# Normalizing one token block from its channel-major copy instead of transposing it

## The chip, the cores and the metric

The kernel runs on one core of a Trainium2 chip. The metric is the device time of one execution in microseconds; a kernel's time is the median over its runs. The engines are called TensorE (PE), VectorE (DVE), ScalarE (ACT), GpSimd (POOL) and SyncE (SP, which issues the transfers).

## What is computed

The input `x` has 2048 tokens of 640 channels. Everything is float32.

```python
xn = layernorm(x)                       # per token, over the 640 channels
qkv = xn @ wqkv                         # 32 heads of 20
phi_q = concat(softmax(q@w_phi), softmax(-(q@w_phi)));  phi_k the same from k
o = phi_q @ (phi_k.T @ v) / (phi_q @ sum(phi_k) + 1e-6)
out = x + o @ wo + (gelu(layernorm(xn) @ w1 + b1) @ w2 + b2)
```

The MLP has 1728 hidden features. It normalizes `xn` once more, so a token's row `x - mean` is multiplied by one factor for the MLP (called `ry` in the kernel) and by another for the attention.

## The kernel before

To keep float32 accuracy, each operand of a large product is split into a high part (rounded to float32r) and a low part (the rest), and a product is three matmuls: high by high, high by low, low by high. This is `mm3`, lines 64 to 66 of the profile; `split` (lines 55, 57 and 58) makes the parts, the high one mostly on ACT, the low one on DVE or POOL.

The 2048 tokens are four blocks of 512. The kernel begins with the MLP of blocks 0 and 1. For a block `b`, `y[b]` holds the normalized tokens with channels on the 128 partitions: five chunks of 512 columns, each as a high and a low part. The weights come in 14 groups of 128 hidden features, `wc[c]` for the first four; a call of `passes(g, b, ...)` takes two such groups (j = 0 and 1) and one block through the MLP:
- its first half, `first`: for each j five `mm3` (chunks `kc` of `y[b]`) into one bank of the matmul memory, then GELU on ACT into `gts` (tile m4) and the split of the result into `hh` and `hl`;
- its second half: for m = 0 to 4 two `mm3` (`w2` parts by `hh`, `hl`) into one of banks 5, 6, 7 in turn, and DVE adds that bank to `acc[b][:, m]`, which was loaded with the residual `x` with channels on partitions (line 295 in group 0, with a bias, else 297).

The order of work at the start is written out by hand; TensorE, DVE, ACT and POOL each execute their instructions in program order. The tokens of blocks 0 and 1 are loaded as eight tiles `x0`, `x1` of 128 tokens by 640 channels. DVE takes mean and variance (`stats`, lines 130 to 154; `mv` holds means, `ry` the factors). ACT subtracts the mean (`centre`, line 158), DVE or ACT multiplies by the factor (`scale`, lines 162 and 164), and `make_y01` transposes each 128x128 piece on TensorE (line 173) into a bank that is then split into `y`. Block 0 goes first in two halves of 256 tokens: `half_first` (line 336) multiplies each half by the first two weight groups as soon as it is there, and `zs` are the four half GELUs that follow, whose results are `hid` of `p00`.

Then the passes are interleaved, so that TensorE always has a product that depends on nothing recent: `p10` (group 1, block 0) first half, `p00` (group 0, block 0) second half, `p01` (group 0, block 1) first half, `p10` second half, and so on. `p01` is the first to read `y[1]`.

A generator `mlp.beside` is advanced by one step after each `mm3`. Here it is `next_y`: after the ninth product group of `p10` it makes `y[1]` from `x1`, one transposed bank for each two further steps, so its 20 transposes stand in groups of 4, 4, 2, 4, 4, 2 among the matmuls of `p10` and `p00`. The `w2` parts of weight groups 0 and 1 are made just before (`parts[c][1]`: high part on DVE, low part on POOL), those of groups 2 and 3 behind `p00` (ACT and POOL).

Of the kernel before, what the change touches and what calls it, by code (L numbers as in the profile page):

```python
# [8 lines left out]
F32 = mybir.dt.float32  # L9
F32R = mybir.dt.float32r  # L10
AF = mybir.ActivationFunctionType
ALU = mybir.AluOpType
# [3 lines left out]
P = 128  # L16
S, D, F, H, DH = 2048, 640, 1728, 32, 20
KC = D // P
# [22 lines left out]
def f(ap):  # L41
    return ap.bitcast(F32)
# [3 lines left out]
def tile_kernel(ctx: ExitStack, tc: tile.TileContext, x, xT, wkT, wqT, wv, wphi, wo, w1, b1, w2, b2,  # L46
                ident, mmask, emask, vsel, out):
    nc = tc.nc
    ctx.enter_context(nc.allow_low_precision(reason="float32 operands are split exactly into float32r parts"))

    def split(hi, lo, src, scale=None, eng=nc.vector, first=nc.scalar):

        if scale is None:
            if first is nc.scalar:
                nc.scalar.activation(hi, src, AF.Copy)  # L55
            else:
                first.tensor_copy(hi, src)
            eng.tensor_tensor(lo, src, f(hi), op=ALU.subtract)  # L58
        else:
            nc.scalar.activation(hi, src, AF.Copy, scale=scale)  # L60
            nc.vector.scalar_tensor_tensor(lo, src, scale, f(hi), op0=ALU.mult, op1=ALU.subtract)
# [8 lines left out]
    idt = cp.tile([P, P], F32, name="idt")  # L70
# [3 lines left out]
    mv = cp.tile([P, 16, 2], F32, name="mv")  # L74
    ry = cp.tile([P, 16], F32, name="ry")
# [14 lines left out]
    acc = [None] * NB  # L90
# [6 lines left out]
    class Banks:  # L97

        def __init__(self, *ids):
            self.ids, self.n = ids, 0  # L100
# [11 lines left out]
    def mtile(i, dtype=F32):  # L112
        return mp.tile([P, 2, D if i < 5 else 512], dtype, name=f"m{i}")
    y = {}

    def load_x(ts, xp, tag="xb"):
        xbs = []
        for t in ts:
            xb = xp.tile([P, D], F32, name=tag)
            nc.sync.dma_start(xb, x[t * P:(t + 1) * P, :])  # L120
            xbs.append(xb)
        return xbs

    def stats(ts, xp, xbs, turned=False):

        t0, n = ts[0], len(ts)
        st = xp.tile([P, n, 2, 6], F32, name="st", bufs=2)
        for i, (t, xb) in enumerate(zip(ts, xbs)):
            for h in range(2):
                nc.vector.bn_stats(st[:, i, h, :], xb[:, h * 320:(h + 1) * 320])  # L130
            nc.vector.bn_aggr(mv[:, t, :], st[:, i, :, :])
            yield


        ts = slice(t0, t0 + n)
        q = xp.tile([P, 2, n], F32, name="q", bufs=2)
        nc.vector.tensor_scalar(q[:, 1, :], mv[:, ts, 1], 0.25 * (1 + EPS), 0.25 * EPS * EPS, op0=ALU.mult, op1=ALU.add)
        nc.vector.tensor_scalar(q[:, 0, :], mv[:, ts, 1], 0.25, 0.25 * EPS, op0=ALU.mult, op1=ALU.add)
        yield

        sr = xp.tile([P, 2, n], F32, name="sr", bufs=2)
        rr = xp.tile([P, 2, n], F32, name="rr", bufs=2)
        nc.scalar.activation(sr, q, AF.Sqrt)
        nc.vector.reciprocal(rr, sr)
        nc.vector.tensor_tensor(rr, rr, q, op=ALU.mult)
        if turned:
            nc.vector.scalar_tensor_tensor(sr, sr, -1.0, rr, op0=ALU.mult, op1=ALU.subtract)
        else:
            nc.vector.tensor_tensor(sr, sr, rr, op=ALU.add)
        nc.vector.reciprocal(ry[:, ts], sr[:, 1, :])  # L150
        yield
        ra = xp.tile([P, n], F32, name="ra", bufs=2)
        nc.vector.reciprocal(ra, sr[:, 0, :])
        nc.vector.tensor_tensor(rs_all[:, ts], sr[:, 1, :], ra, op=ALU.mult)

    def centre(t, xb):

        nc.scalar.activation(xb, xb, AF.Identity, bias=mv[:, t, 0:1], scale=-1.0)

    def scale(t, xb, act=False):  # L160
        if act:
            nc.scalar.activation(xb, xb, AF.Copy, scale=ry[:, t:t + 1])
        else:
            nc.vector.tensor_scalar_mul(xb, xb, ry[:, t:t + 1])

    def make_y01(b, half, xbs, ptile):

        cols = slice(half * 256, half * 256 + 256)
        for c0, n in ((0, 2), (2, 2), (4, 1)):
            ps = ptile()  # L170
            for c in range(n):
                for i in range(2):
                    nc.tensor.transpose(ps[:, c * 256 + i * P:c * 256 + (i + 1) * P],
                                        xbs[i][:, (c0 + c) * P:(c0 + c + 1) * P], idt)
            src = ps[:, :n * 256].rearrange("p (c t) -> p c t", c=n)
            cs = slice(c0, c0 + n)
            split(y[b][0][:, cs, cols], y[b][1][:, cs, cols], src)
            yield
# [20 lines left out]
    class Mlp:  # L199
        def __init__(self, slots, hid):  # L200
            self.hid, self.turn, self.slots, self.beside, self.raw = hid, 0, slots, iter(()), {}
            self.ph, self.px, self.po = Banks(0, 1, 2), Banks(3, 4), Banks(5, 6, 7)

        def fetch(self, c, pool=None):

            for p in self.fetch_parts(c, pool):
                p()
# [42 lines left out]

        def gelu(self, g, j, pz, gt, hh, hl):
            self.last = nc.scalar.activation(gt, pz, AF.Gelu_apprx_tanh, bias=b1t[:, 2 * g + j:2 * g + j + 1]).ins  # L252
            split(hh, hl, gt)

        def passes(self, g, b, ws, hid=None):

# [48 lines left out]
    mlp = Mlp((0, 1, 2, 3), ((0, 2), (1, 3)))  # L305

    def finish(p):
        for _ in p:
            pass

    xs = ExitStack()
    xp = xs.enter_context(tc.tile_pool(name="x01", bufs=8, side="right"))
# [12 lines left out]
    gts = mtile(4)  # L325
    hid = [mtile(2 * j + 1, F32R) for j in range(2)]
    hid = [(h[:, 0, :512], h[:, 1, :512]) for h in hid]
    pall = Banks(5, 6, 7, 3, 4, 0, 1, 5, 2, 6)

    def half_first(half, *order):  # L330

        cols = slice(half * 256, half * 256 + 256)
        pz = [pall()[:, cols] for _ in range(2)]
        for j, wi, yi in order:
            for kc in range(KC):
                nc.tensor.matmul(pz[j], wc[j][wi][:, kc, :], y[0][yi][:, kc, cols],
                                 start=(wi, yi, kc) == (0, 0, 0), stop=(yi, kc) == (1, KC - 1))
        return [lambda j=j: mlp.gelu(0, j, pz[j], *[m[:, cols] for m in (gts[:, j, :512], *hid[j])]) for j in range(2)]

    x1 = load_x(range(4, 8), xp)  # L340
# [14 lines left out]
    s01, s23, s47 = (stats(range(a, b), xp, xbs, True) for a, b, xbs in ((0, 2, x0[:2]), (2, 4, x0[2:]), (4, 8, x1)))  # L355

    def step(gen, n):
        for _ in range(n):
            next(gen, None)
# [22 lines left out]
    scale(2, x0[2])  # L382
    scale(3, x0[3], True)
    zs = half_first(0, *((j, wi, yi) for j in range(2) for wi, yi in ((0, 0), (1, 0), (0, 1))))
    parts[2][0]()
    step(s47, 2)
    step(y23, 4)
    zs += half_first(1, *((j, wi, yi) for ops in (((0, 0), (1, 0)), ((0, 1),)) for j in range(2) for wi, yi in ops))
    for i in range(2):
        centre(4 + i, x1[i])  # L390
    parts[3][0]()
    step(s47, 2)
    step(s01, 1)
    step(s47, 1)
    step(s47, 1)
    for i in range(2, 4):
        centre(4 + i, x1[i])
    for c in range(2):
        parts[c][1](nc.vector)
    for i in range(4):  # L400
        scale(4 + i, x1[i])
        zs[i]()
    for st in (s23, s47):
        step(st, 1)
    p00 = mlp.passes(0, 0, [wc[0], wc[1]], hid)
    next(p00)

    def next_y():
        ptile = Banks(3, 4, 0, 1)
        for _ in range(8):  # L410
            yield
        for half in range(2):
            for _ in make_y01(1, half, x1[2 * half:2 * half + 2], ptile):
                for _ in range(2):
                    yield

    mlp.beside = next_y()
    p10 = mlp.passes(1, 0, [wc[2], wc[3]])
    next(p10)
    finish(p00)  # L420
    for c in range(2, 4):
        parts[c][1]()
    finish(mlp.beside)
    p01 = mlp.passes(0, 1, [wc[0], wc[1]])
    next(p01)
    finish(p10)
# [179 lines left out]
    ptile = Banks(0, 1, 2)  # L606
# [19 lines left out]
    def proj(t, i):  # L626

        yh, yl = y[t // 4]
        c = slice((t % 4) * P, (t % 4) * P + P)
        c0 = CB[i - 1] if i else 0  # L630
        wh, wl = [w[:, :, c0:CB[i]] for w in wkv_] if i < 3 else wq_
        ps = ptile()[:, :wh.shape[2]]
        for kc in range(KC):
            mm3(ps, yh[:, kc, c], yl[:, kc, c], wh[:, kc], wl[:, kc], kc == 0, kc == KC - 1)
        return ps
# [107 lines left out]
    for t, i in [(t, i) for t in range(13) for i in range(4)] + [(13, 0), (13, 1), (13, 2), (14, 0), (14, 1), (13, 3), (14, 2), (15, 0), (15, 1),  # L743
# [6 lines left out]
        ps = proj(t, i)  # L750
# [23 lines left out]
        if i == 0 and t in (1, 2, 3, 6, 7):  # L774

            kc = (1, 2, 3, 6, 7).index(t)
# [7 lines left out]
        if (t, i) == (11, 0):  # L784
            mlp = Mlp((0, 2, 3, 1), ((1, 2), (0, 3)))
# [313 lines left out]
    for g in range(7):  # L1099
        for b in range(2, 4):  # L1100
# [24 lines left out]
            if (g, b) == (0, 3):  # L1125
# [5 lines left out]
                op = ctx.enter_context(tc.tile_pool(name="oB", bufs=1, reuse_waits="tile"))  # L1131
# [55 lines left out]
    step = 0  # L1187
# [133 lines left out]
```

## Time and profile before

| | |
|---|---|
| median of 3 runs | 726.24 us (725.75 to 726.45) |
| the profiled execution: its own time | 725.59 us |
| its span | 723.8 us |
| TensorE busy | 715.3 us, 99% of the span |
| DVE, ACT, POOL busy | 488.0, 333.5, 387.5 us |
| granted TensorE clock | 0.998 of full speed |

An engine's busy time is the time in which it had an instruction under way. In the timeline rows below, the first number is the start in microseconds from the span's start, the second how long the instruction (or a run of like ones) took from start to end; a successor on the same engine may start a little before that end. Behind `x` stands the count. The note in brackets, where there is one, is the idle time of that engine before the row and what ended it.

### The profile page before, as it was taken

The page shows a single profiled execution, that of the slowest core. Times are in us where ns is not written, and L with a number is a line of the kernel's source. Part 1 is how long each engine was busy: PE and PEld are TensorE (multiplying, and loading weights), DVE is VectorE, ACT ScalarE, POOL GpSimd, SP SyncE. Part 2 cuts the span into 40 slices and gives each one's busy share as a digit, 9 for nine tenths or more (in the row PEclk, how much of TensorE's full clock was granted, in tenths as well). Part 3 has the DMA queues.
Part 4 walks back from the last instruction along what each step waited for, and adds up shares of the span by engine and source line. Part 5 has one row for each costly group of instructions (what it writes and reads, how often), then busy time and mean ns, then how long its engine had stood idle before and what let it go on. Part 6 is the DMA issues. An engine that isn't in the chain of part 4 may idle for free.

```text
span 723.8 us, 9764 instructions
## 1 busy us (share of the span) xinstructions
PE 715.3 (99%) x3428; PEld 600.6 (83%) x3428; DVE 488.0 (67%) x821; ACT 333.5 (46%) x567; POOL 387.5 (54%) x342
## 2 busy tenths in 40 slices
PE   8999999999999999999999999999999999999998
PEld 6788888878888888888888888878878888888887
DVE  7847655765544798798788797535565656869753
ACT  7624445433313563463454458336555656551310
POOL 2211222555102896896888878346576786554400
PEclk9999999999999999999999999999999999999999
DMA  9903675555151223624500606873434443163222
GB/s 325 273 21 112 188 203 188 167 185 174 56 219 73 95 74 151 173 91 152 139 1 15 167 1 203 215 205 114 126 107 121 122 142 112 41 230 123 80 81 88
DMA packets 67145, 96.86 MB, mean 134 GB/s; under 512 B 14656, under 2 KB 37840, under 8 KB 65472
## 3 DMA queue, kind: packets, MB, share of 16 engines
q1 hardware_dynamic: 66808, 96.23, 42.9%
q8 instruction: 27, 0.44, 0.2%
q14 instruction: 22, 0.18, 0.1%
q10 hardware_dynamic: 288, 0.01, 0.0%
HBM read 65.87 MB, written 30.35 MB: 133 GB/s over the span
## 4 chain that ended last, share of the span: by engine, by line
PE 85%; DVE 4%; DMA 4%; issue 2%; ACT 2%; POOL 2%; SPq 1%; POOLq 0%; ACTq 0%
PE bank L64 25%; PE bank L65 25%; PE bank L66 25%; PE bank L704 2%; DMA r<-in_w 2%; PE bank L467 2%; PE bank L932 1%; PE bank L931 1%; DMA e<-e 1%; DVE st L130 1%; SPq L737 1%; PE bank L293 1%; PE bank L292 1%; PE bank L273 1%; PE bank L274 1%
## 5 line engine op out<-in xcount | busy, mean ns | idle before, releaser
L58 POOL TENSOR_TENSOR w<-r,w 128x640 fp32r<-128x640 f32 x52 | 84.1, 1636 | 120.0 <-ACT w L55 88.1
L64 PE MATMUL bank<-y,w 128*128 128x512 f32 (+1 forms) x310 | 121.2, 391 | 0.0
L65 PE MATMUL bank<-y,w 128*128 128x512 f32 (+1 forms) x310 | 120.7, 390 | 0.0
L66 PE MATMUL bank<-y,w 128*128 128x512 f32 (+1 forms) x310 | 120.7, 389 | 0.0
L64 PE MATMUL bank<-m,w 128*128 128x512 f32 x266 | 105.7, 397 | 1.1 <-DVE acc L295 0.6
L66 PE MATMUL bank<-m,w 128*128 128x512 f32 x266 | 104.1, 391 | 0.0
L65 PE MATMUL bank<-m,w 128*128 128x512 f32 x262 | 102.4, 391 | 0.0
L58 DVE TENSOR_TENSOR m<-m,m 128x512 fp32r<-128x512 f32 (+1 forms) x54 | 44.9, 832 | 73.8 <-ACT m L55 73.8
L297 DVE TENSOR_TENSOR acc<-bank,acc 128x512 f32<-128x512 f32 x120 | 80.4, 682 | 16.1 <-PE bank L66 11.4
L64 PE MATMUL bank<-wkh,y 128*128 128x512 f32 (+2 forms) x240 | 87.6, 365 | 0.0
L65 PE MATMUL bank<-wkl,y 128*128 128x512 f32 (+2 forms) x240 | 87.1, 363 | 0.0
L66 PE MATMUL bank<-wkh,y 128*128 128x512 f32 (+2 forms) x240 | 86.8, 362 | 0.0
L65 PEld LDWEIGHTS bank<-y,w 128*128 128x128 f32 x310 | 58.7, 189 | 12.3
L66 PEld LDWEIGHTS bank<-y,w 128*128 128x128 f32 x310 | 58.6, 189 | 12.1
L64 PEld LDWEIGHTS bank<-y,w 128*128 128x128 f32 x310 | 58.5, 189 | 12.1
L669 POOL TENSOR_TENSOR m<-m,mx 128x640 f32<-128x640 f32 (+2 forms) x48 | 44.6, 943 | 42.7 <-DVE mx L657 42.7
L650 ACT ACTIVATE m<-bank 128x512 f32<-128x512 f32 (+1 forms) x64 | 26.5, 440 | 85.5 <-PE bank L66 59.6
L925 POOL TENSOR_TENSOR e<-e,m 120x512 fp32r<-120x512 f32 (+1 forms) x28 | 38.0, 1360 | 45.0 <-ACT m L924 44.4
L64 PEld LDWEIGHTS bank<-m,w 128*128 128x128 f32 x266 | 50.0, 188 | 14.3 <-DVE acc L297 3.0
L252 ACT ACTIVATE m<-bank,b1t 128x512 f32<-128x512 f32 (+1 forms) x54 | 36.3, 672 | 52.6 <-PE bank L66 50.1
L66 PEld LDWEIGHTS bank<-m,w 128*128 128x128 f32 x266 | 49.9, 188 | 10.6
L65 PEld LDWEIGHTS bank<-m,w 128*128 128x128 f32 x262 | 49.3, 188 | 10.0
(213 smaller groups left out, 1469.3 us busy)
## 6 DMA issues: line engine op xcount, KB each, us to landing
r<-in_w SPq DMA_DIRECT2D x52, 320.0 KB
e<-e SPq DMA_DIRECT2D x40, 240.0 KB
e<-acc SPq DMA_DIRECT2D x52, 160.0 KB
acc<-in_xT SPq DMA_DIRECT2D x4, 1280.0 KB
xb<-in_x SPq DMA_DIRECT2D x8, 320.0 KB
t<-in_x SPq DMA_DIRECT2D x8, 320.0 KB
raw<-in_xT SPq DMA_DIRECT2D x10, 256.0 KB
yh<-t SPq DMA_DIRECT2D x10, 256.0 KB
```

The costliest lines, as they stand in the source:

```text
L58: eng.tensor_tensor(lo, src, f(hi), op=ALU.subtract)
L64: nc.tensor.matmul(ps, lh, rh, start=first, stop=False, **kw)
L65: nc.tensor.matmul(ps, lh, rl, start=False, stop=False, **kw)
L66: nc.tensor.matmul(ps, ll, rh, start=False, stop=last, **kw)
L130: nc.vector.bn_stats(st[:, i, h, :], xb[:, h * 320:(h + 1) * 320])
L252: self.last = nc.scalar.activation(gt, pz, AF.Gelu_apprx_tanh, bias=b1t[:, 2 * g + j:2 * g + j + 1]).ins
L297: nc.vector.tensor_tensor(acc[b][:, m, :], pw, acc[b][:, m, :], op=ALU.add)
L467: nc.tensor.matmul(ps[:, c + i * kd:c + (i + 1) * kd], raw[n, g][:kk, (kc + i) * P:(kc + i + 1) * P], wpt[:kk, g, :kd // DF, 1:], start=Tr ...
L650: return nc.scalar.activation(p3[:, :, c], ps.rearrange("p (h f) -> p h f", h=H), AF.Copy).ins
L669: subs[n, t] = nc.gpsimd.tensor_tensor(ep[:, s], a, b, op=ALU.subtract)
L704: nc.tensor.matmul(kvp[g // 2][:VM, (g % 2) * 240:(g % 2) * 240 + 240].rearrange("p (s f) -> p s f", s=4), v[:, g * VS:g * VS + VM], ft[:, ...
L925: nc.gpsimd.tensor_tensor(pl, e, f(ph), op=ALU.subtract)
```

## The change

Block 1 is no longer centred, scaled and transposed from `x1`. Its residual copy `acc[1]` already has channels on partitions, so only the 512 means and the 512 factors have to be spread over all partitions. `spread` does this with four transposes: it transposes a column of 128 tokens' values, repeated 128 times, which gives 128 equal rows. ACT copies the spread means to `mb`; POOL takes `ts[c] = mb - acc[1][:, c]` (`minus`); DVE multiplies by the spread factors in bank 2 (`times`) and ACT makes the high part; the low part (`rest`) is made on DVE for chunks 0 to 2 and on POOL for 3 and 4. `minus(0)` stands on POOL ahead of the low parts of `w2` of weight groups 0 and 1, the other four behind them. The half GELUs `zs` follow the first product on DVE. The low parts of `p10`'s two GELU results are held back (`mlp.held`) until `p00` is almost done. Both halves of `half_first` now share banks 3 and 4, and `p01` leaves out bank 2.

```diff
@@ class Mlp
+            self.held = None
@@ gelu
-            split(hh, hl, gt)
+            if self.held is None:
+                split(hh, hl, gt)
+            else:
+                nc.scalar.activation(hh, gt, AF.Copy)
+                self.held.append(lambda: nc.vector.tensor_tensor(hl, gt, f(hh), op=ALU.subtract))
@@ the start
-    pall = Banks(5, 6, 7, 3, 4, 0, 1, 5, 2, 6)
+    pall = Banks(5, 6, 7, 0, 1, 5)
+    zbanks = [Banks(n)() for n in (3, 4)]
@@ half_first
-        pz = [pall()[:, cols] for _ in range(2)]
+        pz = [z[:, cols] for z in zbanks]
@@ after the second half_first
-    for i in range(2):
-        centre(4 + i, x1[i])
     parts[3][0]()
     step(s47, 2)
+    def spread(bank, cols):
+        ps = Banks(bank)()
+        for i in range(4):
+            nc.tensor.transpose(ps[:, i * P:(i + 1) * P], cols[:, i:i + 1].to_broadcast([P, P]), idt)
+        return ps
+    psm, mb = spread(7, mv[:, 4:8, 0]), mtile(5)[:, 0, :512]
+    nc.scalar.activation(mb, psm, AF.Copy)
     step(s01, 1)
     step(s47, 1)
     step(s47, 1)
-    for i in range(2, 4):
-        centre(4 + i, x1[i])
+    ts = [xp.tile([P, D], F32, name="xb")[:, :512] for _ in range(KC)]
+    def minus(c):
+        nc.gpsimd.tensor_tensor(ts[c], mb, acc[1][:, c], op=ALU.subtract)
+    minus(0)
     for c in range(2):
         parts[c][1](nc.vector)
-    for i in range(4):
-        scale(4 + i, x1[i])
-        zs[i]()
-    for st in (s23, s47):
-        step(st, 1)
@@ next_y
-        ptile = Banks(3, 4, 0, 1)
-        for _ in range(8):
-            yield
-        for half in range(2):
-            for _ in make_y01(1, half, x1[2 * half:2 * half + 2], ptile):
-                for _ in range(2):
-                    yield
+        def times(c):
+            nc.vector.tensor_tensor(ts[c], psr, ts[c], op=ALU.mult)
+            nc.scalar.activation(y[1][0][:, c], ts[c], AF.Copy)
+        def rest(c, eng=nc.vector):
+            eng.tensor_tensor(y[1][1][:, c], ts[c], f(y[1][0][:, c]), op=ALU.subtract)
+        for _ in range(3):
+            yield
+        psr = spread(2, ry[:, 4:8])
+        nc.vector.tensor_tensor(ts[0], psr, ts[0], op=ALU.mult)
+        for z in zs:
+            z()
+        nc.scalar.activation(y[1][0][:, 0], ts[0], AF.Copy)
+        mlp.held = []
+        for c in range(1, KC):
+            minus(c)
+        for st in (s23, s47):
+            step(st, 1)
+        yield
+        rest(0)
+        times(1)
+        for _ in range(9):
+            yield
+        rest(1)
+        times(2)
+        yield
+        yield
+        rest(2)
+        times(3)
+        yield
+        times(4)
+        rest(3, nc.gpsimd)
+        rest(4, nc.gpsimd)
+        yield
+        yield
+        mlp.held.pop(0)()
+        yield
+        yield
+        mlp.held.pop(0)()
+        mlp.held = None
@@ before p01
+    mlp.ph.n += 1
```

## Rows read from the trace of the kernel before

**Rows 1.** The page, part 1: busy time, share of the span and instructions.

```profile
PE 715.3 (99%) x3428; PEld 600.6 (83%) x3428; DVE 488.0 (67%) x821; ACT 333.5 (46%) x567; POOL 387.5 (54%) x342
```

**Rows 2.** TensorE's waits over the span: total, times, longest.

```profile
PE bank L64 <- DVE acc L295: 0.6, 1, 0.6
```

**Rows 3.** Timeline of TensorE, 19 to 52 us.

```profile
19.81 0.40 PE L64 MATMUL bank<-y,w 128*128 128x512 f32 x1
...
25.73 0.39 PE L66 MATMUL bank<-y,w 128*128 128x512 f32 x1
...
27.85 0.39 PE L66 MATMUL bank<-m,w 128*128 128x512 f32 x1
...
28.98 0.40 PE L66 MATMUL bank<-m,w 128*128 128x512 f32 x1
...
37.03 0.39 PE L64 MATMUL bank<-y,w 128*128 128x512 f32 x1
...
50.43 0.39 PE L66 MATMUL bank<-m,w 128*128 128x512 f32 x1
```

**Rows 4.** Timeline of GpSimd and VectorE, 15 to 41 us.

```profile
15.26 1.56 POOL L58 TENSOR_TENSOR w<-r,w 128x640 fp32r<-128x640 f32 x1 [2.77 <-ACT w L55]
18.69 1.58 POOL L58 TENSOR_TENSOR w<-r,w 128x640 fp32r<-128x640 f32 x1 [1.88 <-ACT w L55]
...
23.69 1.83 POOL L58 TENSOR_TENSOR w<-r,w 128x640 fp32r<-128x640 f32 x1
...
37.62 3.10 POOL L58 TENSOR_TENSOR w<-r,w 128x640 fp32r<-128x640 f32 x2 [12.10 <-ACT w L55]
...
16.16 1.56 DVE L58 TENSOR_TENSOR y<-bank,y 128x512 fp32r<-128x512 f32 x3
...
19.82 0.46 DVE L154 TENSOR_TENSOR rs_all<-sr,ra 128x2 f32<-128x2 f32 x1
...
21.34 0.18 DVE L150 RECIPROCAL ry<-sr 128x4 f32<-128x4 f32 x1
...
24.37 1.43 DVE L58 TENSOR_TENSOR m<-m,m 128x256 fp32r<-128x256 f32 x1 [0.29 <-ACT m L55]
```

**Rows 5.** Timeline of GpSimd and VectorE around 657 us, one operation each.

```profile
655.44 1.30 POOL L978 TENSOR_TENSOR acc<-acc,rx 128x512 f32<-128x512 f32 x1 [0.75 <-DVE rx L976]
...
656.70 1.74 POOL L978 TENSOR_TENSOR acc<-acc,rx 128x512 f32<-128x512 f32 x1
...
656.49 0.79 DVE L997 TENSOR_TENSOR y<-ob,y 128x512 fp32r<-128x512 f32 x1
...
657.21 1.77 DVE L997 TENSOR_TENSOR y<-ob,y 128x512 fp32r<-128x512 f32 x1
```

**Rows 6.** Timeline of ScalarE, 19 to 33 us.

```profile
22.12 1.28 ACT L252 ACT_TABLE_LOAD   x1
23.41 0.47 ACT L252 ACTIVATE m<-bank,b1t 128x256 f32<-128x256 f32 x1
...
29.61 0.58 ACT L55 ACTIVATE y<-bank 128x512 fp32r<-128x512 f32 x1
30.09 0.68 ACT L252 ACTIVATE m<-bank,b1t 128x512 f32<-128x512 f32 x1
```

**Rows 7.** Timeline of VectorE, 30 to 33 us: operations that read a bank.

```profile
30.34 0.68 DVE L58 TENSOR_TENSOR y<-bank,y 128x512 fp32r<-128x512 f32 x1
...
32.67 0.74 DVE L295 SCALAR_TENSOR_TENSOR acc<-bank,b2t,acc 128x512 f32<-128x512 f32 x1
```

**Rows 8.** Waits of SyncE's issues up to 40 us: total, times, longest.

```profile
SPq L442 <- DMA acc<-in_xT: 2.0, 1, 2.0
```

**Rows 9.** Timeline of SyncE's transfer issues, 19 to 60 us.

```profile
19.30 0.32 SPq L442 DMA_DIRECT2D raw<-in_wkT  x1
...
39.21 0.33 SPq L215 DMA_DIRECT2D r<-in_w  x1
53.99 0.35 SPq L442 DMA_DIRECT2D raw<-in_wkT  x1
```

## What I predict

> **What bounds the kernel now.** I read the page first: TensorE is busy 99% of the span [rows 1], so almost every tenth of a microsecond that the matmul stream gains or loses goes through to the end. Its own waits come next: the one wait for VectorE inside the stage in question is 0.6 us long [rows 2], before an accumulation group that needs its bank back. The third view is TensorE's timeline from 19.8 to 50.4 us [rows 3]. From the first matmul of `p01` (37.03) to the last one of `p10` (50.43) lie 59 intervals, so one 512-column matmul costs 13.40 / 59 = 0.227 us there. From 25.73 (the 27th matmul of `p10`'s first half) to 37.03 there are 34 intervals, which would be 7.72 us and took 11.30: **3.58 us are lost** to the twenty transposes and to waits. That is all the change can win. Of this, a clean group of four transposes costs 28.98 - 27.85 - 3 x 0.227 = 0.45 us, so twenty cost about 2.3 and waits the other 1.3.
>
> **The transposes.** The change leaves eight, in two groups of four: means behind the half-block matmuls, factors behind the fourth product group of `p10`. At 0.45 each this is 0.90 us; the first group also needs the last mean, which DVE has delivered by 19.8, since its `rs_all` operation behind it starts at 19.82 [rows 4], just when TensorE is free (19.81 [rows 3]), so I take 0.48 each: 0.96 us. Their operand is one column repeated 128 times; no row shows such a read. Bounds: the plain transpose, and a whole 512-column matmul (0.227 against 0.11 us each), which adds 8 x 0.12 = 0.9 us. I take the first, since sizes and engine operation are those of the rows. Without any new wait the sum is -3.58 + 0.96 = **-2.6 us**.
>
> **What else leaves and comes.** Four `centre` on ACT, four `scale` on DVE and six high and low parts (ACT 0.58, DVE 0.68 [rows 6, 7]) go. ACT gets a copy of the mean rows and five high parts, DVE five products from PSUM and three low parts, and POOL seven operations that it did not have: five `minus` and two low parts, 1.30 us each by a 128x512 row [rows 5]. So DVE gets no busier. The question is when its work can run.
>
> **VectorE and GpSimd in each other's way.** DVE took 1.43 us for a 256-column subtraction of two SBUF operands at 24.37, ending 0.28 after the POOL operation of 23.69 to 25.52; a two-column multiplication at 19.82 took 0.46 and ended with POOL's at 20.27 [rows 4]. Three operations that read a PSUM bank took 1.56 in all while POOL ran from 15.26 to 16.82 [rows 4], as fast as alone (0.68 for one [rows 7]; one of them has half the columns, and each starts some 0.08 before its forerunner ends). So a DVE operation with both operands in SBUF waits for the running POOL operation; products and accumulations, which read a bank, do not. When both have a queue they take turns: POOL 655.44 to 656.74, DVE to 657.28, POOL (started 656.70) to 658.44, DVE (started 657.21) to 658.98 [rows 5]. Behind POOL's end DVE needs 0.54 us for 512 columns, 0.28 for 256, almost nothing for a few. [...] The Trainium skill (Perfetto Trace Analysis, section "Optimizing Scalar/DVE Operations") warns that moving work between these two engines might not help, for the same reason.
>
> **The schedule that follows.** Before, POOL's operations here ended at 23.69 + 1.83 = 25.52, and it had nothing more until 37.62 [rows 4]. Now it is in one piece from 21 to 33 us:
> - Means transposed by 20.5, copied by ACT (0.58 [rows 6]) until 21.1. `acc[1]` has landed: an issue that waits for that transfer goes out at 19.30 [rows 8, 9]. `minus(0)` is at 21.1 to 22.4.
> - The square root stands behind that copy on ACT, and ends at 21.2; the small multiplication after it waits for `minus(0)`, so the factors are ready at 22.85 instead of 21.34 + 0.18 = 21.52 [rows 4] (an estimate: the four small operations of that chain are about 0.2 apart). TensorE reaches their transposes at 22.9, so that wait is covered, by less than 0.1 us. The two casts end at 23.6, and POOL's second-weight low parts can only follow: 25.2 and 27.0, then `minus(1)` to `minus(4)`.
> - The table load (1.28) and four half GELUs with their copies (0.47 for one, a copy about 0.4, 3.4 in all) end at 25.7 [rows 6]; they cost nothing. But their four low parts on DVE stand between POOL operations. One 1.25 us POOL interval and 0.28 of DVE make 1.53 for each turn, 1.82 behind a weight part: 25.4, 27.3, 28.8, 30.4. The two `rs_all` multiplications, tiny but of two SBUF operands, take the next turns, behind `minus(3)` and `minus(4)`: 31.65 and 32.95.
> - `p00` can start at 19.81 + 30 x 0.227 + 0.96 = 27.6. Its second matmul needs the low parts of both halves, 28.8: **wait 1.0**. The fifth needs the last one, 30.4, and would be due at 29.5: **wait 0.9**.
> - Behind 32.95 DVE has low part 0 (33.55), product 1 (34.15), `acc` m=0 (0.74 [rows 7], until 34.8). TensorE is due at 33.6 with m=3, which takes the same bank 5: **wait 1.25**. Low part 1, product 2 and `acc` m=1 end at 36.75; m=4 is due at 36.2: **wait 0.6**. This is the old 0.6 us wait [rows 2], made longer and doubled.
> - `p01` starts at 38.2 (37.03 before). High part 1 came at 34.8; ACT then has both `p10` GELUs with copies (0.68 for one [rows 6], a copy little less, to 37.3), so high part 2 ends at 37.8, low part 2 at 38.5, product 3 at 39.1, high part 3 at 39.7, POOL's low part 3 at 41.0; TensorE wants it at 40.4: **wait 0.65**. Product 4 and high part 4 end at 41.0; POOL's low part 4, which takes turns with the first held low part, at 42.9, wanted at 41.8: **wait 1.15**.
>
> Waits: 1.0 + 0.9 + 1.25 + 0.6 + 0.65 + 1.15 = 5.55. **Sum: -3.58 + 0.96 + 5.55 = +2.9 us.**
>
> **Edits that cost nothing.** The held low parts end at 41.6 and 43.4, wanted at about 47 in `p10`'s second half; if that cover went, each would cost its 0.7 or so. POOL's low parts of weights 2 and 3 move from 37.62 + 3.10 = 40.7 [rows 4] to about 46.5, wanted at 47.3 and 48.0: less than 2 us of cover, then 1 for 1. The weight fetch that went out at 39.21 goes some 6 us later; SP issued its next at 53.99 [rows 9]. Both block halves in banks 3 and 4, and `p01` in banks 0 and 1, whose GELUs are done by 36.6, meet no reader. After 50 us TensorE stays the bound, so the shift is kept.
>
> **The rivals.**
> 1. *The turns are not strict, or POOL is through before DVE needs the port.* Then the low parts are ready by 28.5, no wait is left, and the time falls by 2.6 us, to about 723.6. Place: DVE's four GELU low parts. It decides if together they lose no more than about one POOL operation (1.3 us). For it: only one clean sequence of alternate turns stands in my rows. Against: nothing else can occupy POOL's place between 23.6 and 33; every operation behind `minus(0)` has its inputs. Chance 0.15.
> 2. *Only the large operations wait, the `rs_all` ones slip between.* Then DVE reaches `acc` m=0 about 2.5 us earlier, the 1.25 wait goes and the others shrink; about 1.8 us come back and +1.1 remains, about 727.3. Against: the two-column row at 19.82. With other partial covers this is a change within 0.2%. Chance 0.15.
> 3. *Alternate turns as above.* +2.9, own range +1.5 to +4.4 (0.9 for the repeated column, 0.5 for seven POOL operations that are 0.07 longer or shorter, short covers). Chance 0.70.
>
> **The numbers.** The profiled execution took 725.59 us with a span of 723.8; it is 0.65 below the median of the runs, 726.24. So a new profiled execution at 728.5, and a median of 726.24 + 2.9 = 729.1. 0.2% (1.45 us) is about what a measurement here can tell from no change: slower 0.70, same 0.15, faster 0.15. The range takes in cases 2 and 3 and leaves out the first: 726.2 to 730.7.
>
> **What would show it.** Right: eight transposes at 0.11 us intervals and none of line 173 behind 20 us; POOL without a gap from 21 to 33 us; 256-column subtractions on DVE of over 1 us each; TensorE waits for DVE's `m` and `acc` and for POOL's `y` that sum to 4 to 6 us before 43; `p01`'s first matmul near 38.2, `p10`'s last near 53.4. Wrong: those subtractions at 0.41, or `p01` starting near 35 us. The prediction also falls if the low parts wait but TensorE's order has slack that I missed, or if the first wait pushes the later ones under its cover more than I counted.

## The result and the profile after

The changed kernel takes 729.55 us (median of 6 runs, 728.86 to 731.25), the kernel before 726.0 us beside it (6 runs, 724.55 to 726.54): ratio 1.0049, 95% interval 1.0035 to 1.0064, so 2.5 to 4.7 us slower. The profiled execution took 728.86 us with a span of 727.1.

The page of the changed kernel, part 1, answers to [rows 1]:

```profile
PE 715.3 (98%) x3416; PEld 599.3 (82%) x3416; DVE 493.8 (68%) x819; ACT 331.4 (46%) x563; POOL 398.1 (55%) x349
```

Twelve transposes are gone, and TensorE still has as many busy microseconds in a longer span. TensorE's waits show two new kinds and, doubled, the one of [rows 2]; these rows are from the list of waits of the changed kernel (total, times, longest):

```profile
PE bank L65 <- POOL y L428: 1.2, 2, 0.7
PE bank L64 <- DVE acc L300: 1.1, 2, 0.8
PE bank L65 <- DVE m L58: 1.0, 2, 0.6
```

Line 428 is `rest`, the low part of `y[1]`; line 58 the low part of a half GELU; line 300 the addition to `acc` (295 before). TensorE's timeline of the changed kernel, against [rows 3]:

```profile
23.01 0.60 PE L402 MATMUL bank<-idt,ry 128*128 128x128 f32 x4
23.36 0.48 PE L64 MATMUL bank<-y,w 128*128 128x512 f32 x1
...
28.55 0.50 PE L65 MATMUL bank<-m,w 128*128 128x512 f32 x1 [0.58 <-DVE m L58]
...
29.96 0.50 PE L65 MATMUL bank<-m,w 128*128 128x512 f32 x1 [0.44 <-DVE m L58]
...
34.24 0.50 PE L64 MATMUL bank<-m,w 128*128 128x512 f32 x1 [0.81 <-DVE acc L300]
...
36.23 0.50 PE L64 MATMUL bank<-m,w 128*128 128x512 f32 x1 [0.33 <-DVE acc L300]
...
37.71 0.39 PE L64 MATMUL bank<-y,w 128*128 128x512 f32 x1
...
40.67 0.50 PE L65 MATMUL bank<-y,w 128*128 128x512 f32 x1 [0.53 <-POOL y L428]
...
42.35 0.50 PE L65 MATMUL bank<-y,w 128*128 128x512 f32 x1 [0.72 <-POOL y L428]
...
52.91 0.39 PE L66 MATMUL bank<-m,w 128*128 128x512 f32 x1
```

The bracket counts from the modelled end of the matmul before. What a wait costs is the distance of two starts less the usual 0.23, and 0.11 at the matmul after it, which also starts late (28.55 to 28.89 is 0.34). So counted, the six waits cost 0.85, 0.72, 1.08, 0.61, 0.80 and 1.00 us: 5.06 in all. `p01` starts at 37.71 (37.03 before) and the last matmul of `p10` stands at 52.91 (50.43): **the stage takes 2.48 us more.** This start of `p10`'s last matmul is the measure of the stage in all that follows.

The reason stands on the other two engines. GpSimd and then VectorE in the changed kernel, against [rows 4]:

```profile
21.11 1.29 POOL L413 TENSOR_TENSOR xb<-m,acc 128x512 f32<-128x512 f32 x1 [2.31 <-ACT m L406]
23.30 3.49 POOL L58 TENSOR_TENSOR w<-r,w 128x640 fp32r<-128x640 f32 x2 [0.89 <-DVE w L57]
26.74 5.56 POOL L413 TENSOR_TENSOR xb<-m,acc 128x512 f32<-128x512 f32 x4
```

```profile
21.40 1.03 DVE L145 TENSOR_TENSOR rr<-rr,q 128x8 f32<-128x8 f32 x1
...
24.33 5.58 DVE L58 TENSOR_TENSOR m<-m,m 128x256 fp32r<-128x256 f32 x4
...
30.02 1.06 DVE L154 TENSOR_TENSOR rs_all<-sr,ra 128x2 f32<-128x2 f32 x1
...
31.20 1.13 DVE L154 TENSOR_TENSOR rs_all<-sr,ra 128x4 f32<-128x4 f32 x1
...
33.45 0.73 DVE L300 SCALAR_TENSOR_TENSOR acc<-bank,b2t,acc 128x512 f32<-128x512 f32 x1
```

Line 413 is `minus`. While GpSimd worked from 23.30 to 32.30, VectorE got one instruction with two SBUF operands through for each of GpSimd's: four low parts in 5.58, and two multiplications of two and four columns in 1.06 and 1.13, which take 0.16 where GpSimd reads nothing (run 3). The accumulation that frees bank 5 ends at 34.18; TensorE wanted the bank at 33.27.

The other 0.8 us of the span's 3.3 come later. Laid matmul by matmul beside the trace of before, the shift is 2.49 us until 130 us, 2.87 behind that and 3.2 from 478 on. The first of these steps is one more turn, far outside the stage. There GpSimd subtracts as soon as a transfer has landed (`raw<-in_xT`), while VectorE has two low parts ahead of an accumulation that frees a bank. GpSimd and the second low part in the kernel before, then in the changed one:

```profile
127.45 1.30 POOL L560 TENSOR_TENSOR raw<-raw,m 128x512 f32<-128x512 f32 x1 [3.89 <-DMA raw<-in_xT]
129.22 0.81 DVE L58 TENSOR_TENSOR wkl<-raw,wkh 128x640 fp32r<-128x640 f32 x1
```

```profile
130.58 1.64 POOL L609 TENSOR_TENSOR raw<-raw,m 128x512 f32<-128x512 f32 x1 [4.54 <-DMA raw<-in_xT]
131.00 1.90 DVE L58 TENSOR_TENSOR wkl<-raw,wkh 128x640 fp32r<-128x640 f32 x1
```

Before, GpSimd started 0.44 us ahead of the first low part (127.89), which waited and took 1.41 us; the second then took 0.81. In the changed kernel GpSimd started 0.21 us behind the first one (130.37), which took 0.69, and the second waited: 1.90. The accumulation starts 2.45 us after the first low part instead of 2.06, so TensorE gets its bank 0.39 us later. The step at 478 us is taken up at the end of the account of the prediction.

### The profile page after: what moved, and what is told of

It reads as the page before. It is cut to its first block, busy times and chain, and to the rows that moved or that the text cites. A ratio compares the mean times of both kernels' runs of the same rounds, so it can differ in the third digit from the quotient of the medians.

```text
span 727.1 us, 9739 instructions
## 1 busy us (share of the span) xinstructions
PE 715.3 (98%) x3416; PEld 599.3 (82%) x3416; DVE 493.8 (68%) x819; ACT 331.4 (46%) x563; POOL 398.1 (55%) x349
## 4 chain that ended last, share of the span: by engine, by line
PE 90%; DVE 4%; DMA 2%; ACT 1%; issue 1%; SPq 1%; POOL 1%; ACTq 0%; DVEq 0%
PE bank L64 27%; PE bank L65 26%; PE bank L66 26%; PE bank L753 2%; PE bank L516 2%; PE bank L981 1%; PE bank L980 1%; DMA e<-e 1%; DVE m L58 1%; PE bank L298 1%; PE bank L297 1%; PE bank L279 1%; PE bank L278 1%; PE bank L342 1%; PE bank L916 1%
## 5 line engine op out<-in xcount | busy, mean ns | idle before, releaser
L58 DVE TENSOR_TENSOR m<-m,m 128x512 fp32r<-128x512 f32 (+1 forms) x52 | 46.6, 901 | 68.8 <-ACT m L55 68.6
```

## The experiments

| run | `p10`'s last matmul, us | against before | median | before on that chip | ratio (95%) |
|---|---|---|---|---|---|
| before, profile shown | 50.43 | | | | |
| before once more | 50.48 | +0.05 | 726.31 (1 run) | 726.46 | |
| after | 52.91 | +2.48 | 729.55 | 726.0 | 1.0049 (1.0035 to 1.0064) |
| 1 small operations late | 51.58 | +1.15 | 729.88 | 726.77 | 1.0041 (1.0023 to 1.0058) |
| 2 GELU kept in its bank | 50.93 | +0.50 | 727.07 | 726.77 | 1.0019 (1.0004 to 1.0035) |
| 3 GpSimd only writes | 48.87 | -1.56 | 725.85 | 726.77 | 0.9992 (0.9977 to 1.0006) |
| 4 no wait left | 47.76 | -2.67 | 724.12 | 726.77 | 0.9977 (0.9959 to 0.9996) |
| 4 again | 47.70 | -2.73 | 724.25 | 726.28 | 0.9977 (0.9964 to 0.9991) |
| 5 before, with added reads | 55.25 | +4.82 | 731.15 | 726.46 | 1.0053 (1.0032 to 1.0075) |
| 6 low parts not held | 55.92 | +5.49 | 733.61 | 726.28 | 1.0099 (1.0083 to 1.0115) |
| 7 last low parts on VectorE | 52.00 | +1.57 | 731.76 (1 run) | 726.46 | |
| 8 `minus` in halves | 50.50 | +0.07 | 728.37 | 726.46 | 1.0014 (0.9997 to 1.0030) |

The stage is read from one profile of each run; two executions of the same kernel differed in it by 0.05 to 0.06 us.

The stage is not the whole of what the change does to the time. The ratio, turned into microseconds of the kernel before, lies 0.9 to 1.8 us above the stage's shift in all eight rows of versions with the change that have a ratio (3.56 for 2.48 in the changed kernel, 2.98 for 1.15 in run 1, 7.19 for 5.49 in run 6), and 1.0 below it in run 5, which is without the change. One interval is about 1 us to either side, and the rows of one chip share their runs of before, so it is the common sign that counts, not a single row.

**1. The two-column operations moved behind the held low parts.**

```diff
-        for st in (s23, s47):
-            step(st, 1)
         yield
         rest(0)
...
         mlp.held = None
+        for st in (s23, s47):
+            step(st, 1)
```

> The two small rs_all multiplications (two and four columns, 0.16 us each when alone) go from the middle of VectorE's queue to its end; nothing else changes. Theory of turns (a VectorE operation with two SBUF operands waits for one whole GpSimd operation): each of them costs a GpSimd operation of about 1.1 us in front of low part 0, product 1 and acc m=0, so the wait for acc m=0 (1.1 us) goes and the one for m=1 shrinks, while both waits for GELU low parts (0.85 and 0.7) and those for low parts 3 and 4 stay: 1.0 to 1.6 us come back of the changed kernel's 3.5, so +1.6 to +2.6 us against the kernel before. Rival (the time is lost because the chain copy, minus, product, high part, low part is longer than the old transposes): 0.3 us of work is moved, no change, +3.5 us.

VectorE in this run:

```profile
24.33 5.58 DVE L58 TENSOR_TENSOR m<-m,m 128x256 fp32r<-128x256 f32 x4
29.84 1.77 DVE L428 TENSOR_TENSOR y<-xb,y 128x512 fp32r<-128x512 f32 x1
...
32.14 0.74 DVE L300 SCALAR_TENSOR_TENSOR acc<-bank,b2t,acc 128x512 f32<-128x512 f32 x1
```

The accumulation starts 1.31 us earlier (32.14 for 33.45), TensorE's wait for bank 5 is gone, that for m = 4 falls from 0.61 to 0.39, and 1.33 us of the stage come back. So two instructions of six columns together had cost 1.3 us, though the low part behind them took one of their two turns (1.77 instead of 0.68). The whole time didn't follow: TensorE's waits for line 302, the accumulation of later groups, total 2.2 us in this trace and 0.8 in the changed kernel's.

**2. The half GELUs written back into their banks.**

```diff
-        return [lambda j=j: mlp.gelu(0, j, pz[j], *[m[:, cols] for m in (gts[:, j, :512], *hid[j])]) for j in range(2)]
+        return [lambda j=j: mlp.gelu(0, j, pz[j], pz[j], *[m[:, cols] for m in hid[j]]) for j in range(2)]
```

> The four half GELUs write their result back into banks 3 and 4, so that their low parts read one operand from a bank and one from SBUF; every operation, its size and its place are as in the changed kernel. Theory of turns: the four low parts no longer wait for GpSimd and are done near 26.1 us, both waits of TensorE for them go, GpSimd's four minus are through 1.1 us earlier, and so are the products and sums behind them; about 0.6 us of wait is left at the low part of chunk 4. Against the kernel before: -1.4 to -2.0 us. Rival (long chain): only the two waits for GELU low parts come back, 1.6 us: about +1.9 us.

VectorE in this run, then ScalarE:

```profile
24.40 0.75 DVE L58 TENSOR_TENSOR m<-bank,m 128x256 fp32r<-128x256 f32 x2
25.75 0.42 DVE L58 TENSOR_TENSOR m<-bank,m 128x256 fp32r<-128x256 f32 x1 [0.60 <-ACT m L55]
26.51 0.42 DVE L58 TENSOR_TENSOR m<-bank,m 128x256 fp32r<-128x256 f32 x1 [0.34 <-ACT m L55]
...
27.04 0.89 DVE L154 TENSOR_TENSOR rs_all<-sr,ra 128x2 f32<-128x2 f32 x1
...
28.05 1.13 DVE L154 TENSOR_TENSOR rs_all<-sr,ra 128x4 f32<-128x4 f32 x1
29.11 1.85 DVE L428 TENSOR_TENSOR y<-xb,y 128x512 fp32r<-128x512 f32 x1
```

```profile
24.85 0.45 ACT L253 ACTIVATE bank<-bank,b1t 128x256 f32<-128x256 f32 x1 [0.71 <-DVE m L58]
```

The same four low parts take 0.42 us or less with one operand in a bank, while GpSimd works: the division by operands holds, and TensorE's two waits for them are gone. The stage won 1.98 us against the changed kernel and is still 0.50 above before, not 1.4 to 2.0 below. The expectation missed two things, and GpSimd was through at 32.11, only 0.19 us earlier and not 1.1. ScalarE's third GELU now waits 0.71 us for VectorE's read of the bank that both halves share. And the queue behind the low parts moved forward into GpSimd's busy time: the same two small operations and the low part of chunk 0 now take the three turns (0.89, 1.13, 1.85), so the accumulation starts at 31.48, only 1.97 earlier.

**3. `minus(1)` to `minus(4)` replaced by fills.** GpSimd writes each whole tile (`full`, 640 columns) twice and reads nothing; the normalization of chunks 1 to 4 of block 1 is left out.

```diff
         for c in range(1, KC):
-            minus(c)
+            for _ in range(2):
+                nc.gpsimd.memset(full[c], 0.01)
```

> minus(1) to minus(4) are left out; in place of each GpSimd fills the 640 columns of that tile twice with a constant, which takes as long but reads nothing, so block 1 is normalized from constants. Theory of turns (only a GpSimd operation that reads SBUF stands in the way): the low parts and small multiplications of VectorE run beside it at 0.41 and 0.16 us, and all waits go but that for the low part of chunk 4, about 1.0 us: -1.0 to -1.9 us against the kernel before. Rival (GpSimd's own time is what is late): as long as in the changed kernel, +3 to +3.5 us. Rival (VectorE and GpSimd block each other whatever GpSimd does): the same, +3 to +3.5 us.

GpSimd and then VectorE in this run:

```profile
26.76 5.12 POOL L441 MEMSET xb<- 128x640 f32 x8
```

```profile
24.36 3.41 DVE L58 TENSOR_TENSOR m<-m,m 128x256 fp32r<-128x256 f32 x4
...
27.88 0.16 DVE L154 TENSOR_TENSOR rs_all<-sr,ra 128x2 f32<-128x2 f32 x1
...
28.16 0.16 DVE L154 TENSOR_TENSOR rs_all<-sr,ra 128x4 f32<-128x4 f32 x1
```

GpSimd is nearly as busy as in the changed kernel (5.12 us for 5.56), but VectorE doesn't notice: 0.16 us for either small operation. The low parts lose time only to the two weight parts that end at 26.8. The first four waits of TensorE are gone, and the stage ends 1.56 us before that of the old kernel. So it is GpSimd's reading that blocks, not its being busy. The Trainium skill (SBUF — State Buffer, section "Who interferes with whom") says the same of an instruction that only writes; this run agrees.

**4. Everything out of GpSimd's way.** The edits of 1 and 2, and the low parts of chunks 3 and 4 on VectorE:

```diff
-        rest(3, nc.gpsimd)
-        rest(4, nc.gpsimd)
+        rest(3)
+        rest(4)
```

> Both edits together (GELUs in their banks, small multiplications last), and low parts 3 and 4 on VectorE in place of GpSimd. Theory of turns: no wait of TensorE is left between 20 and 53 us, only eight transposes in place of twenty: -2.3 to -2.6 us against the kernel before, p01's first matmul near 34.5 us. Rival (long chain): at best what the second edit gives, and VectorE has 1.4 us more to do: 0 to +2 us.

VectorE in this run:

```profile
26.97 1.43 DVE L428 TENSOR_TENSOR y<-xb,y 128x512 fp32r<-128x512 f32 x1
...
29.15 0.75 DVE L300 SCALAR_TENSOR_TENSOR acc<-bank,b2t,acc 128x512 f32<-128x512 f32 x1
...
35.23 1.48 DVE L428 TENSOR_TENSOR y<-xb,y 128x512 fp32r<-128x512 f32 x2
```

TensorE has no wait between 20 and 53 us, and the stage ends at 47.76: 2.67 us less than before, where the prediction's sum without waits was 2.6. By its interval (0.9959 to 0.9996) the version is faster than the kernel before, and so than the changed kernel, whose interval against before lies wholly above 1. Run again on another chip:

> The version without TensorE waits in this stage once more (half GELUs written back into their banks, the two-column operations late, the last two low parts on VectorE), for its interval: its earlier ratio to the kernel before was 0.9977 (0.9959 to 0.9996). If the gain is that of the stage (2.67 us of 726 is 0.37%), the ratio is 0.995 to 0.998 again and p10's last matmul stands at 47.7 to 47.9. If the earlier gain came from a lucky arrival of transfers later in the kernel, the ratio comes back to 0.999 to 1.001, with p10's last matmul at 47.8 all the same.

The stage ended at 47.70 and the ratio was 0.9977 again, now 0.9964 to 0.9991. By the ratio that is 1.7 us, less than the 2.7 of the stage (the medians are 2.65 and 2.03 apart). In both traces the shift against before falls to 2.3 us at 128 us and 1.4 at 476 us, where TensorE waits 1.8 to 1.9 us instead of 0.95 for ScalarE, which waits for a transfer.

**5. The kernel before, with four reads by GpSimd added.** Four 128x512 subtractions of parts of `acc[1]` into an unused tile, behind the two weight parts; nothing else differs.

```diff
+    extra = mtile(5)[:, 0, :512]
...
+    for c in range(4):
+        nc.gpsimd.tensor_tensor(extra, acc[1][:, c], acc[1][:, c + 1], op=ALU.subtract)
```

> The kernel before, with four more GpSimd subtractions of 128x512 behind its two weight parts; they read acc[1] and write a tile that nothing reads. No data depends on them. Theory of turns: the four GELU low parts and three scale operations of VectorE take turns with them; the last-but-one low part is done near 32.1 instead of 27.4 us, the first transposes wait 1.1 us and p00's second matmul another 3.4 us: p10's last matmul near 54.9 instead of 50.43 us, +4 to +5 us. Rival (idle GpSimd time costs nothing): no change, 50.4 us.

VectorE in this run (line 164 is `scale`, of a single SBUF tile):

```profile
25.77 1.56 DVE L164 TENSOR_SCALAR xb<-xb,ry 128x640 f32<-128x640 f32 x1
27.25 1.50 DVE L58 TENSOR_TENSOR m<-m,m 128x256 fp32r<-128x256 f32 x1
...
31.55 0.54 DVE L164 TENSOR_SCALAR xb<-xb,ry 128x640 f32<-128x640 f32 x1
32.01 0.41 DVE L58 TENSOR_TENSOR m<-m,m 128x256 fp32r<-128x256 f32 x1
```

The kernel without any part of the change loses more than the change did, +4.82. The low parts take 1.50 beside GpSimd and 0.41 behind its end at 31.34. `scale` waits too (1.56 and 0.54), although only one of its operands is a whole SBUF tile, the other a column of factors: two whole operands in SBUF aren't the only way to be blocked. The profile of before has such a row of its own, beside GpSimd's two weight parts of 21.98 to 25.52:

```profile
22.22 1.87 DVE L164 TENSOR_SCALAR xb<-xb,ry 128x640 f32<-128x640 f32 x1
```

The prediction sorted VectorE's operations into those with both operands in SBUF and those that read a bank, and left this third kind out. Its sum lost nothing by that, since the four `scale` go with the change.

**6. The low parts of `p10`'s GELUs not held back.**

```diff
-        mlp.held = []
...
-        mlp.held.pop(0)()
...
-        mlp.held.pop(0)()
-        mlp.held = None
```

> The changed kernel with one part taken out: the low parts of p10's two GELU results aren't held back but queued on VectorE where the GELUs are issued. Place: they then stand on VectorE ahead of the accumulation of m = 0, and need ScalarE's results, the second of which ended shortly before 37 us in the changed kernel. Theory (program order on VectorE sets when TensorE gets its bank back): the accumulation of m = 0 comes 3 to 4 us later than 33.45, p00's wait for bank 5 grows from 1.0 to 3 to 5 us, and p10's last matmul stands at 54.9 to 57 (52.91 with holding), so the whole kernel is 2 to 4 us above the changed one, about 732 to 734. Rival (the holding is of no use, since VectorE is free by then or the low parts are queued behind the accumulation anyway): p10's last matmul within 0.3 us of 52.91, the time within 0.2% of 729.6.

VectorE, then TensorE, then its granted clock (the last column but two of the table of windows):

```profile
35.42 0.69 DVE L58 TENSOR_TENSOR m<-m,m 128x512 fp32r<-128x512 f32 x1 [1.99 <-ACT m L55]
36.66 0.69 DVE L58 TENSOR_TENSOR m<-m,m 128x512 fp32r<-128x512 f32 x1 [0.55 <-ACT m L55]
37.27 0.74 DVE L300 SCALAR_TENSOR_TENSOR acc<-bank,b2t,acc 128x512 f32<-128x512 f32 x1
```

```profile
38.07 0.54 PE L64 MATMUL bank<-m,w 128*128 128x512 f32 x1 [4.74 <-DVE acc L300]
38.41 0.63 PE L65 MATMUL bank<-m,w 128*128 128x512 f32 x1
38.83 0.63 PE L66 MATMUL bank<-m,w 128*128 128x512 f32 x1
```

```profile
39.00:40.00 1.00, 1.00 (x4) 0.81 (x3) 0.96 (x3) 0.63 (x1) 0.00 (x0) 0.50 0.00 0
```

The two low parts stand ahead of the accumulation and wait for ScalarE; the accumulation ends at 38.0 and TensorE waits 4.90 us for bank 5. So the holding is worth 3.01 us of the stage (55.92 for 52.91): 3.93 more at this wait, 8 matmuls with 0.20 us more each behind it, less the 2.4 us of the three later waits, which this one covers (and the stage began 0.07 earlier). The whole kernel, 733.61, is within what was expected too.

**7. Only the last two low parts on VectorE** (the third edit of 4 alone).

> Low parts 3 and 4 of block 1 go from GpSimd (1.3 us each) to VectorE (0.69 us), nothing else. Theory: of the last two waits (0.8 and 1.0 us), that for part 3 is shortened by some 0.3 and that for part 4 goes, since GpSimd's operation was the longest link behind the high part: p10's last matmul near 51.6 instead of 52.91 us. Rival (VectorE is the full engine there): the sums acc m=3 and m=4 come later and the gain is eaten: 52.9 or later.

The wait for chunk 3 falls from 0.80 to 0.61 and that for chunk 4 from 1.00 to 0.09; the stage gives back 0.91 (a new wait of 0.15 stands at 49.4). The run's time, 731.76, says nothing of it: its trace has a wait of 4.0 us at 482 us for ScalarE and a transfer.

**8. `minus(1)` to `minus(4)` in halves of 256 columns.**

```diff
-    def minus(c):
-        nc.gpsimd.tensor_tensor(ts[c], mb, acc[1][:, c], op=ALU.subtract)
+    def minus(c, n=2):
+        for i in range(n):
+            s = slice(i * 512 // n, (i + 1) * 512 // n)
+            nc.gpsimd.tensor_tensor(ts[c][:, s], mb[:, s], acc[1][:, c, s], op=ALU.subtract)
...
-    minus(0)
+    minus(0, 1)
```

> minus(1) to minus(4) on GpSimd in two halves of 256 columns each: the same elements, twice the instructions. Theory of turns (a waiting VectorE operation gets the port behind one GpSimd instruction, however long): each turn behind a minus is 0.6 us shorter, the last GELU low part is done near 28.8 instead of 29.8 us and acc m=0 near 32.3 instead of 34.2, so the waits of 0.85, 0.7, 1.1 and 0.6 shrink to less than 1.0 in all, and those for low parts 3 and 4 stay: p10's last matmul near 50.5 instead of 52.91 us. Rival (the two engines share the port in proportion, or GpSimd's total time decides): GpSimd is not sooner through, 52.9 or slightly later.

GpSimd, then VectorE:

```profile
26.57 7.14 POOL L415 TENSOR_TENSOR xb<-m,acc 128x256 f32<-128x256 f32 x8
```

```profile
24.18 4.46 DVE L58 TENSOR_TENSOR m<-m,m 128x256 fp32r<-128x256 f32 x4
...
28.75 0.50 DVE L154 TENSOR_TENSOR rs_all<-sr,ra 128x2 f32<-128x2 f32 x1
...
29.37 0.58 DVE L154 TENSOR_TENSOR rs_all<-sr,ra 128x4 f32<-128x4 f32 x1
```

GpSimd needs 1.6 us more for the same columns, and VectorE's turns are half as long: 0.50 and 0.58 for 1.06 and 1.13. The work is the same and so are both orders; only the grain of GpSimd's instructions differs. The waits for the GELU low parts shrink to 0.28 and 0.18, that for bank 5 is gone, and the stage is at +0.07.

That this is the 50.5 us expected is in part two misses that cancel. GpSimd now works until 33.71 instead of 32.30, so the low part of chunk 1 takes a turn as well (1.25 us at 31.86; 0.69 in the changed kernel). The accumulation behind it comes later, and TensorE waits 1.13 us for the bank of m = 4 instead of 0.61:

```profile
34.42 0.50 PE L64 MATMUL bank<-m,w 128*128 128x512 f32 x1 [0.86 <-DVE acc L300]
```

So the first four waits came to 1.59 us, not to less than 1.0. On the other side the wait for chunk 3, expected to stay at 0.80, fell to 0.16.

## Why the prediction held, step by step

- **The transposes.** Forecast 0.48 us a group, 0.96 in all. A group costs 0.35 (23.01 to 23.36) and 0.09 at the second matmul behind it, 0.44, so 0.88. Of the two bounds for the repeated column the lower was right: four take 0.60 us, and the group's cost is within 0.01 of the plain one's 0.45.
- **The sum without waits, -2.6.** Run 4 shows it by itself: -2.67 and -2.73.
- **The waits.** All six stand where the schedule put them, each for the instruction that it named. Forecast 1.0, 0.9, 1.25, 0.6, 0.65, 1.15 (5.55); measured 0.85, 0.72, 1.08, 0.61, 0.80, 1.00 (5.06). The term that was off is the turn: 5.58 / 4 = 1.40 us for a 256-column low part, not 1.53, and 1.06 and 1.13 for the small operations, not a whole 1.25 and 1.30 (an instruction of VectorE that waits already doesn't wait for the whole of GpSimd's). `p01` therefore started at 37.71, not 38.2; the later waits came to 1.80 in all, as forecast.
- **The factors.** The small multiplication behind `minus(0)` took 1.03 us and the factors were ready at 22.84 (forecast 22.85). Their transposes started at 23.01, one usual interval after the matmul before, so the cover of less than 0.1 us held. GpSimd idled 0.89 us before the first weight part (the row of 23.30), as in the schedule; the sign "without a gap" was too strict.
- **The stage.** Forecast +2.9, `p10`'s last matmul at 53.4; measured +2.48 and 52.91. What followed, "the shift is kept", was wrong: it grew to 3.3 in the span and 3.55 between the medians. Its schedule of turns ends at 43 us, and one more stood at 130 us (0.39 us). That the median lies so near the forecast is in part chance: a stage 0.4 smaller and a rest 0.8 to 1.1 larger.
- **Rival 1** (the turns aren't strict) fell: the four low parts took 1.40 each, not 0.41. **Rival 2** (the small ones slip between) fell too, by the rows of 1.06 and 1.13 and by run 1, which got 1.33 us back by moving them; the rival had priced that at 1.8. **Alternate turns** stand on runs 3 (no reading, no waits), 2 (a bank operand, no waits), 8 (half the grain, half the turn) and 5 (the reading alone, without the change).
- **Edits at no cost.** The held low parts ended at 41.16 and 42.85 and no matmul waited for them. What the prediction didn't price is what holding saves: 3.0 us (run 6).

What isn't settled is what moves these later waits. The step near 130 us is a turn, and it is 0.36 to 0.39 us in all nine profiles of versions with the change; counted in the same way, run 5 has none and the kernel before, run once more, 1.36. At 478 us TensorE waits for ScalarE, which waits for transfers (`e<-e`). Counted from TensorE's matmuls, SyncE issues the first of them 0.6 to 1.4 us later than before in all nine, and the shift grows there by 0.3 to 4.0 us; in run 5 and the kernel before, run once more, it issues it within 0.02 us of before, and the shift doesn't grow. That is a sign that a part of this step belongs to the change. What delays the issue, no run isolated.

## What to carry to other kernels

Before moving work to GpSimd, list what VectorE has queued in that stretch with both operands in SBUF (by run 5 also a multiplication of an SBUF tile by a column), however small: beside GpSimd instructions that read SBUF each pays for about one of them, and what stands behind it on VectorE (here the accumulation that frees a bank) pays for all of them. The cures that the runs priced are to move tiny instructions out of the stretch (1.3 us of the stage here), to leave one operand in its bank (2.0), and to cut GpSimd's instructions shorter (2.4, for 1.6 us of GpSimd's own time). Each has to be followed one step further, since the next instruction, freed of one turn, moves forward into another (runs 2 and 8). And turns far behind the stage belong in the list too: the one at 130 us changed though nothing there was edited.

## What had not been expected

- **A long wait costs more than itself.** The granted clock is 1.00 in the changed kernel's stage, whose waits are at most 0.97 us. Behind the 4.90 us wait of run 6 it is 0.50 from 39 to 41 us (1.2 GHz, the lower level), and 512-column matmuls start every 0.43 us instead of 0.23: 1.6 us more. Run 5 has the same behind a wait of 2.98 us.
- **Waits that move from one execution to the next.** The kernel before, run once more, waited 1.66 us at 132 us for VectorE and 1.46 at 492, where the profile of before has 0.30 and none, and its shift of 1.4 us was given back from 477 us on, where ScalarE waits for a transfer (5.2 us there, 6.2 in the first profile, 7.1 in run 4). So the times of one kernel scatter by 1 to 4 us with nothing changed, and a stage's own last matmul, steady within 0.06 us, tells more of the stage than the time of one run. What the change does behind the stage shows only when several profiles of either kind are laid side by side.
